# Two-chunk attention blocks: first AV phases ahead of the second scores, from chunk 8 on, with later loads held back

## The chip, the cores and the metric

The kernel runs on one core of one Trainium2 chip. The metric is the device time of one execution in microseconds; the profile is one execution of its own, taken by the hardware profiler.

## The reference

Eight batches of eight heads with 576 positions and 64 channels: causal attention in which each position sees itself and the 63 before it, then, on the heads put side by side (4608 tokens of 512 channels), a gated feed-forward network with 1536 hidden units.

```python
scores = scale * np.matmul(q, k.transpose(0, 1, 3, 2))
mask = (rel >= 0) & (rel < window)            # rel = i - j, window = 64
attn = softmax(np.where(mask, scores, -1e9))
x = (attn @ v) laid out as (B * S, H * D)     # 4608 x 512
out = (silu(x @ w_gate) * (x @ w_val)) @ w_out
```

Inputs and output are float32; the kernel works in bfloat16 with float32 sums.

## The kernel before

**Order of work.** The program is written out by hand as one list of operations, each for one engine; `_Graph` (L32) finds from the tiles read and written which operation waits for which, and gives each engine its operations in the order of the list. A wait on the own engine is made only where the list asks for it with `after=`. A DMA takes one of 16 lanes of its queue (POOL and SP have 16 each, ACT 8) and waits for the lane's DMA before it.

**Tiling.** The 4608 tokens are 36 chunks of 128 tokens. Four chunks make one of nine feed-forward groups c of 512 tokens. A chunk n passes through:

- `load` (L307), on POOL: q and k of chunk n into rings `qn`, `kn` of eight, v into a ring `va` of ten, from float32 to bfloat16 on the way. A chunk that crosses a batch's border takes two DMAs for each.
- `T` (L349), on SP: DMA transposes of kn and qn into rings `kT`, `qT` of eight chunks. Chunks 4 to 9 are loaded by `load2` and transposed on TensorE by `T2` instead.
- scores: `Sx` (L600) gives `Sb` for chunks under 18 (24 small matmuls: L419, L423) and `Sk` from 18 on (16 or more: L468); each takes a pair of PSUM banks, and two exponentials on ACT write `pt` (L431, L477). `Sm` (L436) multiplies `pt` by the mask on DVE.
- attention times v, AV: `AVa` (L511) takes a pair of banks; `AVp` (L606) issues phase 0 or phase 1, some 32 matmuls of 64x64 each way (L535 in `AVmm` for chunks under 18, L498 in `AVk` from 18 on). Phase 1 adds to what phase 0 left in the same banks and is given `after=done[0]`, the operation of phase 0 of the same chunk. `AVn` (L571) divides by the row sums on DVE (L577, L580) into `xb`.
- `X` (L623): transposes `xb` into `xT`, by an SP DMA (L632), or with "act" by TensorE and an ACT copy.
- `F` (L682): for hidden tile f, four matmuls with the gate weights and four with the value weights (L702), a tanh on ACT (L708) and two DVE operations (L710, L712) into `hT`. All F of group c need xT of its chunks 4c to 4c + 3; some F of groups 0 and 1 do a half or a quarter of the tokens.
- `O` (L718): twelve matmuls of 512 columns (L738), a copy on ACT and the store on ACT's queue. `O2` (L723) does the same as two halves of 256 columns in two banks, copied by ACT and DVE, with the store called later.

**PSUM.** There are eight banks. At first two fixed rings serve; once `lru` is set (L930, just before chunk 12's block) `bank` takes the least recently touched bank and `pair` the neighbouring pair whose later touch is oldest. "Touched" counts operations of the list.

**Blocks.** `B(n)` (L590), a single-chunk block: phase 0 of n, scores of n + 1, phase 1 of n. Chunks 8 to 15 go through it (L907 to L937), chunk 8's and 17's scores stand alone (L901, L947), and F, O and X lie between the blocks. `B2(n)` (L609), a two-chunk block: scores n + 2, phase 0 of n, scores n + 3, phase 0 of n + 1, then phase 1 and AVn of n, then of n + 1, then the masks. The loop for groups 3 to 8 (L950) calls B2 at u = 0 and u = 2, each after two F and an O2; after it come the store, X of both chunks, the transposes T of k for n + 4 and n + 5 and of q for n + 5 and n + 6, the loads of q and k for n + 7 and n + 8, then of v for n + 2 and n + 3. Loads wait only for buffers and lanes, so POOL runs far ahead of the other engines.

Of the kernel before, what the change touches and what calls it, by code (L numbers as in the profile page):

```python
# [11 lines left out]
NFC = T // 512  # L12
# [141 lines left out]
class _Kernel:  # L154
# [149 lines left out]
        g.op("dve", lambda e: e.tensor_copy(k[64:128, 0:64], m[64:128, 64:128]), reads=["mask"], writes=[("kmask", 1)])  # L304
        g.op("dve", lambda e: e.tensor_copy(k[64:128, 64:128], m[64:128, 0:64]), reads=["mask"], writes=[("kmask", 2)])

    def load(self, n, what="kqv"):  # L307
        if n >= NCH:
            return
        parts = list(self.segs(128 * n, 128))  # L310
        for x in what:
            src = {"k": self.k, "q": self.q, "v": self.v}[x]
            if x == "v":
                dst, nm, i = self.va[n % self.NV], "va", n % self.NV
            else:
                i = n % self.NQ
                dst = (self.kn if x == "k" else self.qn)[i][:, :].rearrange("p (h d) -> p h d", h=H)
                nm = x + "n"
            for j, (r, b, s, L) in enumerate(parts):
                d = dst[r:r + L, :, 0:64]  # L320
                a = src[b, :, s:s + L, :].rearrange("h p d -> p h d")
                ks = [(nm, i, j)] if len(parts) > 1 else [(nm, i, 0), (nm, i, 1)]
                self.g.op("pool", lambda e, d=d, a=a: e.dma_start(d, a), writes=ks, dma=True)  # L323

    def load2(self, st, x):
        src, dst = (self.k, self.ks2[st % 2]) if x == "k" else (self.q, self.qs2[st % 2])
# [281 lines left out]

    def B2(self, n):  # L609
        ss = [m for m in (n + 2, n + 3) if m < NCH]  # L610
        st = []
        for i in range(2):
            if i < len(ss):
                self.Sx(ss[i])
            st.append(self.AVa(n + i))
            self.AVp(st[i], 0)
        for a in st:
            self.AVp(a, 1)
            self.AVn(a)
        for m in ss:  # L620
            self.Sm(m)
# [96 lines left out]
    def O(self, c, u):  # L718
        io = (4 * c + u) % self.NO
        self.Omm(c, u, 0, 512, "act", [("ost", io), ("osth", io)])  # L720
        self.store(c, u)

    def O2(self, c, u):  # L723
        io = (4 * c + u) % self.NO
        self.Omm(c, u, 0, 256, "act", [("osth", io)])
        self.Omm(c, u, 256, 512, "dve", [("ost", io)])

    def Omm(self, c, u, lo, hi, eng, wr):
        g = self.g
        ih = c % self.NH  # L730
        hT = self.hT[ih]
        ost = self.ost[(4 * c + u) % self.NO]
        OB, ok = self.bank("f")
        n = hi - lo

        def pe(e):
            for f in range(NF):
                r = e.matmul(OB[:, 0:n], hT[:, f, 128 * u:128 * u + 128], self.Wo[:, f, lo:hi],  # L738
                             start=(f == 0), stop=(f == NF - 1))
            return r  # L740

        g.op("pe", pe, reads=self.hTk(ih) + [("Wo", f) for f in range(NF)], writes=[ok])
        self.copy(eng, ost[:, lo:hi], OB[:, 0:n], [ok], wr)
# [57 lines left out]
    def late_loads(self):  # L801
        self.load2(4, "k")
        self.load2(4, "q")
        self.load_wo(0, 6)
        self.load_wo(6, 12)
        self.load(10, "kq")
        self.load(8, "v")
        self.load(11, "kq")
        self.load(9, "v")

    def Tkq(self, n):
        self.T(n, "k")
# [2 lines left out]
    def build(self):  # L815
        F, S, AV, X, T2, O = self.F, self.S, self.AV, self.X, self.T2, self.O
        self.loads()
        self.banks("a", [4, 5, 6, 7, 0, 1, 2, 3, 4, 5, 0, 1, 2, 3, 4, 5, 6, 7, 0, 1, 2, 3, 4, 5, 6, 7, 6, 7])
        self.warm(72, n=80)
        self.first_T(("dve", "act"))  # L820
        s0 = self.Sa(0)
        T2(0, "q", ("act", "dve"))
        self.Sbias(s0)
        self.warm(2)
        self.Sb(s0)
        s1 = self.Sa(1, True)
        self.Sb(s1)
        T2(1, "k", ("dve", "act"))
        T2(1, "q", ("dve", "act"))
        self.early_loads()  # L830
        s2, s3 = self.Sa(2), self.Sa(3)
        a0, a1, a2, a3 = self.AVa(0), self.AVa(1), self.AVa(2), self.AVa(3)
        self.AVs(a0)
        self.shift(1, 0, "dve")
        self.AVn(a0)
        self.Sbias(s2)
        self.Sb(s2)
        self.AVs(a1)
        self.AVn(a1)
        self.Sbias(s3)  # L840
        self.Sb(s3)
        X(0, "dve", "a")
        X(1, "dve", "a")
        self.warm(1, j=2)
        self.AVs(a2)
        self.AVn(a2)
        self.AVs(a3)
        self.AVn(a3)
        F(0, (0, 1), 0, 256)
        X(2, "act", "a")  # L850
        X(3, "act", "a")
        F(0, (2, 3), 0, 256)
        F(0, (0, 1), 256, 512)
        self.banks("a", [4, 5, 6, 7])
        self.init_va(4, self.NV)
        self.more_loads()
        F(0, (2, 3), 256, 512)
        F(0, (4,))
        F(0, (5,))
        F(0, (6,))  # L860
        T2(2, "k", ("act", "act"))
        T2(2, "q", ("act", "act"))
        self.late_loads()
        F(0, (7,))
        S(4)
        F(0, (8,))
        self.B(4)
        F(0, (9,))
        X(4, "act")
        T2(3, "k", ("act", "act"))  # L870
        F(0, (10,))
        a5 = self.AVa(5)
        self.AVmm(a5, 0)
        T2(3, "q", ("act", "act"))
        self.AVmm(a5, 1)
        self.AVn(a5)
        F(0, (11,))
        X(5, "act")
        F(1, (0, 1), 0, 128)
        S(6)  # L880
        F(1, (0, 1), 128, 256)
        F(1, (2, 3), 0, 256)
        self.B(6)
        F(1, (4, 5), 0, 256)
        X(6, "act")
        T2(4, "k", ("act", "act"))
        F(1, (6, 7), 0, 256)
        a7 = self.AVa(7)
        self.AVmm(a7, 0)
        T2(4, "q", ("act", "act"))  # L890
        self.AVmm(a7, 1)
        self.AVn(a7)
        self.load(12, "kq")
        self.load(10, "v")
        for n in range(10, 12):
            self.Tkq(n)
        O(0, 0)
        X(7, "act")
        self.load(13, "kq")
        self.load(11, "v")  # L900
        S(8)  # L901
        O(0, 1)
        self.load(14, "kq")
        self.load(12, "v")
        self.Tkq(12)
        F(1, (0, 1), 256, 512)
        self.B(8)  # L907
        X(8)
        self.Tkq(13)
        F(1, (8,))  # L910
        self.load(15, "kq")
        self.load(13, "v")
        F(1, (2, 3), 256, 512)
        self.B(9)
        X(9)
        self.Tkq(14)
        F(1, (9,))
        O(0, 2)
        F(1, (10,))
        self.B(10)  # L920
        self.load(16, "kq")
        F(1, (4, 5), 256, 512)
        F(1, (11,))
        X(10, "act")
        self.B(11)
        self.load(17, "kq")
        O(0, 3)
        X(11, "act")
        F(1, (6, 7), 256, 512)
        self.lru = True  # L930
        self.init_kmask()
        for u in range(4):
            n = 12 + u
            for m in ((18,), (19, 20), (21,), (22,))[u]:
                self.load(m, "kq")
            self.load(n + 2, "v")
            self.B(n)  # L937
            X(n)
            for m in ((15, 16), (17,), (18,), (19,))[u]:
                self.Tkq(m)  # L940
            if u == 3:
                self.T(20, "q")
            F(2, (3 * u,))
            F(2, (3 * u + 1,))
            O(1, u)
            if u == 3:
                self.Sx(17)  # L947
                self.Sm(17)
            F(2, (3 * u + 2,))
        for c in range(3, NFC):  # L950
            for u in range(4):
                n = 4 * c + u + 4
                F(c, (3 * u,))
                F(c, (3 * u + 1,))
                two = n < NCH and u % 2 == 0
                if two:
                    self.O2(c - 1, u)
                elif n < NCH or u < 3:
                    O(c - 1, u)
                if two:  # L960
                    self.B2(n)
                    self.store(c - 1, u)
                    X(n)
                    X(n + 1)
                    for m in (n + 4, n + 5):
                        self.T(m, "k")
                    for m in (n + 5, n + 6):
                        self.T(m, "q")
                    for m in (n + 7, n + 8):
                        self.load(m, "kq")  # L970
                    for m in (n + 2, n + 3):
                        self.load(m, "v")
                F(c, (3 * u + 2,))
                if n >= NCH and u == 3:
                    O(c - 1, u)
        for u in range(3):
            O(NFC - 1, u)
        self.O_last(NFC - 1, 3)
        self.g.emit()
# [42 lines left out]
```

## Time and profile before

| what | us |
|---|---|
| median of three runs (lowest, highest) | 334.62 (333.92, 335.17) |
| the profiled execution | 335.11 |
| its span, first to last instruction | 333.1 |
| TensorE (PE) busy | 324.1 |
| weight loads (PEld) busy, beside PE | 181.7 |
| VectorE (DVE) busy | 207.2 |
| ScalarE (ACT) busy | 134.4 |
| POOL busy | 107.0 |

| DMA queue | packets | MB | share of 16 engines |
|---|---|---|---|
| q0, loads from POOL | 109008 | 18.62 | 78.2% |
| q1, transposes from SP and the first load | 42848 | 10.63 | 22.2% |
| q10, stores from ACT | 5456 | 9.57 | 8.1% |
| q8, instructions | 28 | 0.46 | 0.6% |

TensorE's granted clock is 1.00 throughout. Starts in the trace are counted from the span's start. A row of a timeline names start, length, engine, line, operation, tiles and count; the bracket at its end is the idle time before it and what ended that, where "issue" means that the profile names nothing. A row of a windows table names the stretch and its length, then busy time and count for each engine asked for, the granted clock, the mean share of the DMA engines and GB/s.

### The profile page before, as it was taken

Reading aid. Unit: us, or ns where it says so; the run is one execution under the profiler, and the core shown is the slowest. Engines: PE = TensorE matmul, PEld = TensorE weight load, DVE = VectorE, ACT = ScalarE, POOL = GpSimd, SP = SyncE. Lnnn points to the kernel's source line nnn. Section 1 sums busy time; section 2 is a strip of 40 time slices with the busy share of each in tenths; the row PEclk is TensorE's granted clock in tenths of the full one; section 3 lists DMA queues with packets and bytes.
Section 4 is the critical chain, followed back from the end, with each engine's and each line's share of the span. In section 5 each row is a group of like instructions: output and inputs, shape, how many; then the busy total and the mean of one; then the engine's idle time right before and its main releaser. Section 6 shows DMA issues by size and latency. Waiting matters only on the chain.

```text
span 333.1 us, 8426 instructions
## 1 busy us (share of the span) xinstructions
PE 324.1 (97%) x3615; PEld 181.7 (55%) x3615; DVE 207.2 (62%) x365; ACT 134.4 (40%) x243; POOL 107.0 (32%) x137
## 2 busy tenths in 40 slices
PE   7899999998999999999999999999999999999996
PEld 6585586655544455555555464646464646444444
DVE  4676884666666658575757575757666667555520
ACT  2645764644433444342424242434342422233221
POOL 8899977644226320607060830100000000000000
PEclk9999999999999999999999999999999999999999
DMA  9999999999999998969996997541423211100012
GB/s 139 178 191 185 177 200 155 173 137 153 173 161 176 158 147 118 151 92 134 124 150 104 137 166 112 81 96 50 110 63 81 59 40 49 48 31 33 31 61 97
DMA packets 157348, 39.34 MB, mean 118 GB/s; under 512 B 144384, under 2 KB 152832, under 8 KB 157312
## 3 DMA queue, kind: packets, MB, share of 16 engines
q0 software_dynamic: 109008, 18.62, 78.2%
q1 hardware_dynamic: 42848, 10.63, 22.2%
q10 hardware_dynamic: 5456, 9.57, 8.1%
q8 instruction: 28, 0.46, 0.6%
q14 instruction: 8, 0.07, 0.1%
HBM read 37.75 MB, written 9.44 MB: 142 GB/s over the span
## 4 chain that ended last, share of the span: by engine, by line
PE 92%; POOL 2%; DMA 2%; issue 1%; ACT 1%; DVE 1%; POOLq 0%
PE ps L702 56%; PE ps L738 28%; DMA va<-in_v_dram 2%; PE ps L498 2%; PE ps L535 2%; PE ps L468 2%; POOL vs L257 1%; PE ps L372 1%; PE ps L423 1%; PE ps L419 1%; PE ps L639 1%; POOL qs L332 1%; ACT kT L255 0%; ACT qT L255 0%; POOL ks L332 0%
## 5 line engine op out<-in xcount | busy, mean ns | idle before, releaser
L710 DVE SCALAR_TENSOR_TENSOR uu<-sig,ps 128x512 bf16<-128x512 bf16 (+1 forms) x109 | 74.0, 679 | 69.2 <-ACT sig L708 69.1
L702 PE MATMUL ps<-xT,Wg 128*128 128x512 bf16 (+2 forms) x488 | 111.4, 355 | 0.4 <-issue 0.4
L702 PE MATMUL ps<-xT,Wv 128*128 128x512 bf16 (+2 forms) x488 | 111.2, 355 | 0.0
L738 PE MATMUL ps<-Wo,hT 128*128 128x256 bf16 (+1 forms) x564 | 99.0, 329 | 1.3 <-issue 1.3
L708 ACT ACTIVATE sig<-ps 128x512 bf16<-128x512 f32 (+1 forms) x109 | 64.9, 596 | 79.2 <-PE ps L702 78.9
L738 PEld LDWEIGHTS ps<-Wo,hT 128*128 128x128 bf16 x564 | 54.9, 98 | 41.7 <-issue 1.8
L712 DVE SCALAR_TENSOR_TENSOR hT<-uu,ps 128x512 bf16<-128x512 bf16 (+1 forms) x109 | 74.3, 682 | 3.8
L702 PEld LDWEIGHTS ps<-xT,Wv 128*128 128x128 bf16 x488 | 47.1, 98 | 46.3
L702 PEld LDWEIGHTS ps<-xT,Wg 128*128 128x128 bf16 x488 | 44.8, 98 | 42.8 <-issue 0.8
L255 ACT ACTIVATE ost<-ps 128x512 f32<-128x512 f32 (+1 forms) x36 | 19.2, 532 | 83.3 <-PE ps L738 83.3
L323 POOL DMA_DIRECT2D kn<-in_k_dram x29 | 25.0, 869 | 72.8 <-DMA kT<-kn 68.0
L323 POOL DMA_DIRECT2D va<-in_v_dram x40 | 34.8, 893 | 19.6 <-PE ps L498 17.9
L323 POOL DMA_DIRECT2D qn<-in_q_dram x29 | 25.0, 872 | 10.9 <-DMA va<-in_v_dram 3.5
L580 DVE TENSOR_TENSOR xb<-ps,rc 128x512 bf16<-128x512 f32 x36 | 24.9, 692 | 1.2
L477 ACT ACTIVATE pt<-ps 128x512 bf16<-128x512 f32 x36 | 18.6, 602 | 11.6 <-PE ps L468 11.6
L431 ACT ACTIVATE pt<-ps 128x512 bf16<-128x512 f32 x36 | 19.4, 595 | 9.2 <-PE ps L423 8.8
L257 DVE COPY ost<-ps 128x256 f32<-128x256 f32 x11 | 4.7, 425 | 26.2 <-PE ps L738 26.2
L445 DVE TENSOR_TENSOR pt<-pt,mask 128x1024 bf16<-128x1024 bf16 x14 | 9.6, 684 | 8.6 <-ACT pt L431 8.6
L577 DVE RECIPROCAL rc<-ps 128x8 f32<-128x8 f32 x36 | 7.3, 203 | 7.6 <-PE ps L498 5.6
L445 DVE TENSOR_TENSOR pt<-pt,kmask 128x1024 bf16<-128x1024 bf16 x18 | 11.5, 683 | 0.0
L535 PE MATMUL ps<-va,pt 64*64 64x65 bf16 x448 | 8.9, 196 | 0.6 <-issue 0.5
L498 PE MATMUL ps<-va,pt 64*64 64x65 bf16 x544 | 9.1, 194 | 0.0
(59 smaller groups left out, 136.9 us busy)
## 6 DMA issues: line engine op xcount, KB each, us to landing
out_dram<-ost ACTq DMA_DIRECT2D x35, 256.0 KB, 3.0
va<-in_v_dram POOLq DMA_DIRECT2D x32, 128.0 KB, 7.8
kn<-in_k_dram POOLq DMA_DIRECT2D x23, 128.0 KB, 11.3
qn<-in_q_dram POOLq DMA_DIRECT2D x23, 128.0 KB, 10.8
Wg<-in_moe_w_gate_dram POOLq DMA_DIRECT2D x6, 256.0 KB, 7.4
Wv<-in_moe_w_val_dram POOLq DMA_DIRECT2D x6, 256.0 KB, 6.8
Wo<-in_moe_w_out_dram POOLq DMA_DIRECT2D x2, 768.0 KB, 14.4
qs<-in_q_dram POOLq DMA_DIRECT2D x3, 256.0 KB, 6.7
```

The lines of the kernel that those rows point to most:

```text
L255: self.g.op("act", lambda e: e.activation(d, a, ACTF.Copy), reads=reads, writes=writes)
L323: self.g.op("pool", lambda e, d=d, a=a: e.dma_start(d, a), writes=ks, dma=True)
L431: g.op("act", lambda e, po=po, p=p: e.activation(po, sv[p], ACTF.Exp, scale=SCALE), reads=[bx[p][1]], writes=[pk[p]])
L445: self.g.op("dve", lambda e: e.tensor_tensor(pt, pt, m, ALU.mult), reads=pk + mk, writes=pk)
L477: g.op("act", lambda e, po=po, p=p: e.activation(po, sv[p], ACTF.Exp, scale=SCALE), reads=[bx[p][1]], writes=[pk[p]])
L498: x = e.matmul(av[64 * c:64 * c + 64, p, j, :], pt[rows, h, x0:x0 + 64], vv[rows, h, 0:65], start=first, stop=phase == 1, skip_group_check ...
L580: g.op("dve", lambda e: e.tensor_tensor(xo, av[:, :, :, 0:64], rb, ALU.mult), reads=bk + [("rc", ir)], writes=[("xb", ix, 0), ("xb", ix, 1)])
L702: r = e.matmul(bank[:, a * n:a * n + n], W[:, kk, f * 128:f * 128 + 128], xT[:, kk, lo:hi], start=(kk == 0), stop=(kk == NK - 1))
L708: g.op("act", lambda e, G=bank: e.activation(sig[:, 0:w], G[:, 0:w], ACTF.Tanh, scale=0.5), reads=[bk], writes=[("sig", i)])
L710: g.op("dve", lambda e: e.scalar_tensor_tensor(uu[:, 0:w], sig[:, 0:w], 1.0, G[:, 0:w], ALU.add, ALU.mult), reads=[("sig", i), gk], writes ...
L712: g.op("dve", lambda e: e.scalar_tensor_tensor(out, v3(uu), 0.5, v3(V), ALU.mult, ALU.mult), reads=[("uu", i), vk], writes=[("hT", ih, f) ...
L738: r = e.matmul(OB[:, 0:n], hT[:, f, 128 * u:128 * u + 128], self.Wo[:, f, lo:hi], start=(f == 0), stop=(f == NF - 1))
```

## The change

1. `B2` issues scores n + 2, phase 0 of n and of n + 1, then scores n + 3, then both second phases. It also keeps phase 0 of chunk n as `gate`.
2. `O2` takes its two banks as a pair.
3. Chunks 8 to 15 go through B2: scores 8 and 9 stand together, the blocks of 8 and 10 are written out in group 1's part, each after an O2, and the loop begins with group 2. Bank choice by age and the mask for later chunks (`init_kmask`) are set before O(0, 0).
4. Loads of q, k, v: chunks 12 and 13 (q, k) and 10 and 11 (v) move up into `late_loads`; later ones are given `after=gate`. In the loop the loads of v come ahead of those of q and k.

```diff
     def B2(self, n):
         ss = [m for m in (n + 2, n + 3) if m < NCH]
-        st = []
-        for i in range(2):
-            if i < len(ss):
-                self.Sx(ss[i])
-            st.append(self.AVa(n + i))
-            self.AVp(st[i], 0)
+        if ss:
+            self.Sx(ss[0])
+        st = [self.AVa(n), self.AVa(n + 1)]
+        for a in st:
+            self.AVp(a, 0)
+        self.gate = st[0][3][0]
+        if len(ss) > 1:
+            self.Sx(ss[1])
         for a in st:
             self.AVp(a, 1)
             self.AVn(a)
...
     def O2(self, c, u):
         io = (4 * c + u) % self.NO
-        self.Omm(c, u, 0, 256, "act", [("osth", io)])
-        self.Omm(c, u, 256, 512, "dve", [("ost", io)])
+        bx = self.pair()
+        self.held -= {b[1][1] for b in bx}
+        self.Omm(c, u, 0, 256, "act", [("osth", io)], bx[0])
+        self.Omm(c, u, 256, 512, "dve", [("ost", io)], bx[1])
```

In `build`, after the second phase of chunk 7, the new order is:

```python
        self.gate = a7[3][0]
        for n in range(10, 12):
            self.Tkq(n)
        self.lru = True
        self.init_kmask()
        O(0, 0)
        X(7, "act")
        S(8)
        S(9)
        O(0, 1)
        for n in (14, 15):
            self.load(n, "kq", self.gate)
        F(1, (0, 1), 256, 512)
        for n in range(12, 14):
            self.Tkq(n)
        F(1, (8,))
        self.O2(0, 2)
        self.B2(8)
        self.store(0, 2)
        X(8)
        X(9)
        for n in (12, 13):
            self.load(n, "v", self.gate)
        for n in (16, 17):
            self.load(n, "kq", self.gate)
        F(1, (2, 3), 256, 512)
        F(1, (9,))
        F(1, (4, 5), 256, 512)
        self.O2(0, 3)
        self.B2(10)
        self.store(0, 3)
        for n in (14, 15):
            self.Tkq(n)
        self.T(16, "q")
        self.load(18, "kq", self.gate)
        F(1, (10,))
        X(10, "act")
        F(1, (6, 7), 256, 512)
        X(11, "act")
        F(1, (11,))
        for c in range(2, NFC):
```

The loop's body is as before but for the loads:

```diff
+                    for m in (n + 2, n + 3):
+                        self.load(m, "v", self.gate)
                     for m in (n + 7, n + 8):
-                        self.load(m, "kq")
-                    for m in (n + 2, n + 3):
-                        self.load(m, "v")
+                        self.load(m, "kq", self.gate)
```

## The prediction

> **What bounds the kernel now.** I read the page's busy shares first, then its slices and the chain that ended last, and then the timeline and the windows around each stretch that the change touches.
>
> ```profile
> PE 324.1 (97%) x3615; PEld 181.7 (55%) x3615; DVE 207.2 (62%) x365; ACT 134.4 (40%) x243; POOL 107.0 (32%) x137
> ...
> PE   7899999998999999999999999999999999999996
> ...
> DMA  9999999999999998969996997541423211100012
> ...
> PE 92%; POOL 2%; DMA 2%; issue 1%; ACT 1%; DVE 1%; POOLq 0%
> ```
>
> TensorE is busy for 97% of the span and makes 92% of the chain, so only what lengthens or shortens its stream counts. The DMA row is the second thing to see: the transfer engines are full up to slice 16 (about 130 us) and nearly idle afterwards. The changed blocks of chunks 8 to 15 (62 to 117 us) lie in the full part, the loop's blocks from chunk 16 on in the idle part.
>
> A full TensorE can still stand. In the timeline of PE:
>
> ```profile
> 78.28 1.47 PE L738 MATMUL ps<-Wo,hT 128*128 128x512 bf16 x6
> 81.01 1.47 PE L738 MATMUL ps<-Wo,hT 128*128 128x512 bf16 x6 [1.26 <-issue]
> ...
> 119.40 0.38 PE L702 MATMUL ps<-xT,Wg 128*128 128x512 bf16 x1 [0.39 <-issue]
> ```
>
> The first stop is in the middle of one group of twelve matmuls, which waits for nothing of the program. Its predecessor is at 53.6 us, in the middle of a second AV phase. Up to these two points TensorE's trace has 1,729 and 2,497 records (matmuls, weight loads, waits): 768 apart, three times 256. The page's queue q8 (kind "instruction") has 28 packets of 16 KB for 7,331 such records, 262 each. One of those packets begins at 51.96 and one at 78.46, and TensorE resumes 2.3 and 2.55 us later. So these are **waits for the next block of 256 instructions**; starts of single matmuls put the second at 1.42 us above the usual pitch. The stop at 119 us is another kind: F(3, 0) needs xT of chunk 15, whose transpose by SP was issued at 112.25 and landed at 119.31; against the pitch it costs 0.55 us.
>
> **The change, part by part.** *Reordering B2.* Windows of PEld in the block of chunk 18 (us, busy, count):
>
> ```profile
> 142.49:143.55 1.06, 0.96 (x72) 1.00 0.18 11
> 143.55:143.63 0.08, 0.00 (x0) 1.00 0.00 0
> 143.63:143.89 0.26, 0.22 (x17) 1.00 0.00 0
> ```
>
> The empty row is the second AV phase of chunk 19, held by done[0] until the first phase of chunk 19 has drained; only chunk 18's second phase lies between. From start to start this gap is 0.13 to 0.17 us in the nine blocks of chunks 16 to 32, 1.38 in sum; an unforced one is 0.004. After the change the scores of n+3 and a phase lie between, so the wait goes: at most -1.35. What is late next: the four bank pairs of a block are used in the order scores, AV, scores, AV; now the second scores take the fourth pair, by the least-recently-touched rule that of O2. DVE's copy of O2's second half ends 0.53 us after the block's start (142.69 + 0.42), and with 0.05 us of signalling the pair is free at 0.58; scores (0.25) and two AV phases (0.13 each) with a switch bring TensorE there at about 0.52. I charge 0.06 a block, 0.5 in all: **-0.8**, bounds -1.35 and 0 (should the wait be as long as the one removed). The last block has no scores and stays.
>
> *Two-chunk blocks for 8 to 15.* Windows of PE: one single block, one lone scores group, one two-chunk block:
>
> ```profile
> 109.85:110.59 0.74, 0.74 (x57) 1.00 1.84 147
> 116.71:117.19 0.48, 0.48 (x26) 1.00 1.06 63
> 125.47:126.91 1.44, 1.44 (x98) 1.00 1.53 97
> ```
>
> Before: eight single blocks and two lone scores (8 and 17), 8 x 0.74 + 2 x 0.48 = 6.88. After: scores 8 and 9 together (0.48 + 0.25) and four blocks of 1.44 - 0.16 + 0.06 = 1.34: 6.09. Four more projections become O2, 24 half-width matmuls in 2.62 us for 12 in 2.59: +0.12. Sum **-0.67**; bounds -0.9 and -0.3.
>
> *The stop at 119 us.* X(14) and X(15) are now issued after the block of 14, two F and one O before F(3, 0), with about 7.3 us in hand beyond X(15)'s issue where 7.1 were short by a little; the loads then in flight are the question (a rival below). **-0.55**.
>
> *Loads.* POOL issues one load in 0.88 us; loads from 14 on now wait for a first AV phase, which on POOL delays all behind it. Needed dates: scores 10/11 at 66.9 (kT/qT 11 landed 64.4 in the profile), 12/13 at 76 (here about 73), 14/15 at 89 (about 86), so 2.5 to 4 us of cover; the order of SP (T 12 and 13, X 8 and 9, T 14 on) keeps them, and X(8), X(9), landing near 79, are needed by F(2, 0) at 83. If a transfer took 4 us longer, each such date would stop TensorE by what exceeds the cover. V of 12 and 13 is issued at 67 and needed at 89. Cost **0**, bounds 0 and +1.5. init_kmask's three small DVE copies and the bank rule move 30 us ahead beside a DVE that is 0.7 busy there: 0.
>
> *Instruction blocks.* This is the term that costs. The change packs TensorE's short instructions: a two-chunk block has 224 of them in 1.3 us, O2 has 48 where O has 24. Counting on from the stop at 53.6 (record 1,729; the next borders are at 1,985, 2,241, 2,497), I take a block as asked for 296 records before its border, since from 125 us on the packets begin 0.4 to 1.9 us after that record; between 45 and 115 us they begin 3.9 to 6.1 us after it (mean 5.0), and at the stops use came 2.3 to 2.5 us later still. The profiled kernel took 10.9 us over the 296 records before 2,241 and 6.7 over those before 2,497, which was 1.4 too few. Laid out with the new order, the request for 2,241 falls eight instructions into O2(0, 2), at 64.6; then come the block of 8 (224 instructions), one F and border 2,241 at 69.8: 5.2 us against 6.2 to 8.6. I take the delay of the row nearest in time (4.36, the packet at 66.8): 4.4 + 2.4 + 0.2 = 7.0, a stop of 1.8. The next, 2,497, lies inside the block of 10, 7.1 us after that stop's end; its packet, counted from there as the one at 86.43 came 5.4 after the resumption at 81.01, needs 6.2 to 8.6, 7.5 in the middle: 0.5. Together 2.3 instead of 1.42: **+0.9**, bounds -1.4 (no stop) and +3.8.
>
> The Trainium skill, "Runtime: NRT & Kernel Launch", section "Instruction fetch mechanics", says that instructions come in 16 KiB blocks of 256 through the sequencer's own DMA queue, and that the cost of crossing a border is mostly hidden. The block size agrees with the trace's 768 = 3 x 256; "mostly hidden" does not hold at 53.6 and 79.4 us, where 0.5 and 1.42 us show. By that sentence the two stops of the new order would be absent and the sum 2.3 lower.
>
> *Transposes beside loads:* +0.1 (below). **Sum**: -0.8 - 0.67 - 0.55 + 0.9 + 0.1 = -1.0. The profiled execution took 335.11 us, 333.1 of span and 2.0 around it; this makes 334.1. It lay 0.5 above the median of 334.62, so for a median I forecast **333.6**.
>
> **Rivals.** *A, instruction blocks arrive in time:* held-back loads leave the transfer queue emptier, and a packet begins within 1 us as it does after 125 us. For it: DMA is then idle from about 86 to 89 us. Against it: at 64 to 76 us the loads of 11, 14 and 15, four transposes and a store are still to move. 333.6 - 2.3 = 331.3.
>
> *B, slower: X collides with the held-back loads.* In the idle part the loads used to start after SP's kT transposes, some 8 us into a block's period; now they start at the first AV phase, 2.8 us before X(n+1). Landing of X's transposes (min/median/max), first 50 to 80 us, then 125 to 230 us:
>
> ```profile
> DMA to landing us min/median/max: 8.7/8.8/9.0
> ...
> DMA to landing us min/median/max: 2.4/3.1/5.9
> ```
>
> In blocks with u = 2, F(c+1, 0) needs X(n+1) 7.3 us after its issue. It decides from that point: at 9.0 us each of the four blocks that still load (14, 18, 22, 26) stops for 1.7, +6.8: 340.3. Against it: the nearest rows beside fresh loads are 5.9 (X at 195.7 us) and 6.8 (qT at 185.2), inside the 7.3. The Trainium skill, "DMA: Bandwidth & Descriptors", section "Queues, rings and completion order", has each engine go round between its queues packet by packet, which speaks against a transpose waiting for whole loads; 8.8 against 3.1 us in the trace shows that it waits for much all the same.
>
> *C, the reordering gives nothing:* the second scores wait for O2's copies as long as the phase did. 333.6 + 0.8 = 334.4.
>
> *D, slower: both instruction blocks come at the late end,* 3.5 and 1.7 us of stop instead of 1.8 and 0.5: 333.6 + 2.9 = 336.5.
>
> **How the numbers follow.** Forecast 0.47 (332.3 to 335.0 of its own), A 0.25, C 0.10, D 0.10, B 0.08. The range runs from A's 331.3, less 0.3 for a run's scatter, to 335.6, part of the way to D: 331.0 to 335.6 leaves out B, most of D and A's tail. 0.5%, about what a measurement of this kernel can tell from no change, is 1.67 us: faster (below 332.95) is A and 0.10 of the forecast, 0.35; slower (above 336.3) is B and half of D, 0.13; the same 0.52.
>
> **What would show it.** Right: in two-chunk blocks no empty stretch of PEld before the last AV phase, and blocks near 1.30 to 1.34 us; F(3, 0) without a stop; a stop near 70 us 256 records before the old one at 2,497. Wrong: no "issue" stop between 64 and 80 us (A); stops at F(4, 0), F(5, 0) ended by xT's transposes (B); an empty stretch ahead of the second scores (C); stops over 3 us (D).

## The result and the profile after

| | median us (lowest, highest) | runs | ratio to before (95%) |
|---|---|---|---|
| before | 333.99 (333.09, 335.54) | 20 | |
| after | 335.83 (333.88, 337.56) | 20 | 1.0047 (1.0026 to 1.0067) |

The kernel became slower by 0.5%; 333.6 was forecast, range 331.0 to 335.6. Its executions spread over 3.7 us where those of before spread over 2.5. They come in two kinds: ten have a mean granted clock of 0.990 to 0.995 and a median of 336.8 us, ten one of 0.999 or 1.00 and a median of 334.3. The profiled execution of the changed kernel, one of the first kind, took 336.66 us with a span of 334.9, 1.8 more than before.

The page of the changed kernel, busy shares and slices:

```profile
PE 325.5 (97%) x3663; PEld 186.9 (56%) x3663; DVE 210.0 (63%) x369; ACT 132.9 (40%) x243; POOL 107.1 (32%) x137
...
PEclk9999999989999999999999999999999999999999
...
DMA  9999999999999898979896959596949352100012
```

The number of matmuls rose by 48, as it must for four more O2, and no engine became the bound. New is the 8 in the row PEclk, the clock that TensorE was granted. The DMA row shows the held-back loads: the full part now has gaps and reaches further into the loop.

The timeline of PE around that 8, in the changed kernel:

```profile
69.15 0.82 PE L704 MATMUL ps<-xT,Wv 128*128 128x256 bf16 x6
72.25 0.39 PE L704 MATMUL ps<-xT,Wv 128*128 128x256 bf16 x2 [2.29 <-issue]
```

The stop stands in the middle of a group of sixteen matmuls, at record 2,241 of TensorE's stream, the border that the prediction named, 69.7 us where it had said 69.8. The packet of instructions began 5.05 us after the record taken for its request and TensorE resumed 2.55 us after the packet's start: 2.34 us above the pitch where 1.8 had been forecast. The prediction had no line for what follows. Windows of PE (us, busy and count, granted clock, DMA share, GB/s):

```profile
66.71:70.12 3.41, 3.26 (x129) 1.00 1.61 179
70.12:73.53 3.41, 1.27 (x7) 1.00 2.14 143
73.54:76.95 3.41, 3.41 (x14) 0.50 3.40 133
```

From 73.54 to 76.95 us the clock is granted at one half. In that row PE is busy throughout, with 14 matmuls, and those of 512 columns start 427 ns apart where they started 216 apart before it. It does in 3.41 us what it else does in 1.71: **1.7 us** on the path for a stop that was already over. The cut into rows of 3.41 us is the profile's own: the clock's record before it lasts 68.27 us, 20 times 3.413.

The two profiled executions, term by term in us (from starts of single instructions in both traces):

| | forecast | measured |
|---|---|---|
| order inside B2, nine blocks from 16 on | -0.8 | -0.70 |
| two-chunk blocks for 8 to 15, with four more O2 | -0.67 | -0.31 |
| stop before F(3, 0) | -0.55 | -0.55 |
| X late at F(5, 0) and F(6, 0) | +0.1 | +0.53 |
| standing for instruction blocks at 64 to 80 us | +0.9 | +0.92 |
| clock at one half afterwards | not thought of | +1.71 |
| up to O(0, 0) | 0 | +0.18 |
| sum | -1.0 | +1.78 |

The sum is the difference of the spans. It holds for these two executions: the term of the clock is missing in the ten whose clock did not fall. Two windows of PE, the blocks of chunks 18 and 8 in the changed kernel, show the first two terms:

```profile
144.37:145.67 1.30, 1.30 (x90) 1.00 0.00 0
...
66.84:68.27 1.43, 1.43 (x115) 1.00 1.48 194
```

The first took 1.40 before. The second has replaced two single blocks of 0.74, and had been put at 1.34.

### The profile page after: what moved, and what is told of

It is laid out like the page before. It is cut to its first block, busy times and chain, and to the rows that moved or that the text cites. A ratio compares the mean times of both kernels' runs of the same rounds, so it can differ in the third digit from the quotient of the medians.

```text
span 334.9 us, 8502 instructions
## 1 busy us (share of the span) xinstructions
PE 325.5 (97%) x3663; PEld 186.9 (56%) x3663; DVE 210.0 (63%) x369; ACT 132.9 (40%) x243; POOL 107.1 (32%) x137
## 4 chain that ended last, share of the span: by engine, by line
PE 91%; POOL 3%; DMA 2%; issue 1%; ACT 1%; DVE 1%; POOLq 0%
PE ps L704 55%; PE ps L742 28%; DMA Wv<-in_moe_w_val_dram 2%; PE ps L468 2%; PE ps L498 1%; PE ps L535 1%; POOL va L323 1%; PE ps L419 1%; PE ps L372 1%; POOL qs L332 1%; POOL Wg L338 0%; PE ps L423 0%; PE ps L641 0%; ACT kT L255 0%; ACT qT L255 0%
## 5 line engine op out<-in xcount | busy, mean ns | idle before, releaser
L742 PEld LDWEIGHTS ps<-Wo,hT 128*128 128x128 bf16 x612 | 59.7, 98 | 36.4
L255 ACT ACTIVATE ost<-ps 128x512 f32<-128x512 f32 (+1 forms) x36 | 18.3, 509 | 77.3 <-PE ps L742 77.3
L257 DVE COPY ost<-ps 128x256 f32<-128x256 f32 x15 | 6.4, 425 | 32.2 <-PE ps L742 32.2
L423 PE MATMUL ps<-qT,kT 64*64 64x64 bf16 x288 | 7.9, 195 | 0.5 <-issue 0.5
L535 PE MATMUL ps<-va,pt 64*64 64x65 bf16 x448 | 7.5, 194 | 0.5 <-issue 0.4
```

The costliest lines, as they stand in the source:

```text
L255: self.g.op("act", lambda e: e.activation(d, a, ACTF.Copy), reads=reads, writes=writes)
L535: x = e.matmul(av[64 * c:64 * c + 64, p, j, :], pt[rows, h, 64 * c:64 * c + 64], vv[rows, h, 0:65], start=first, stop=phase == 1, skip_gro ...
```

## The experiments

Theory 1: the loss is the wait for a block of instructions at 70 us and the halved clock that it brings; what the prediction said of the rest holds. Theory 2: the held-back loads cost the time. Theory 3: the new order of the blocks costs it. In the names, a_ is a variant of the changed kernel and b_ of the kernel before. The medians of before in the four sets were 334.1, 334.0, 334.7 and 334.0.

**Moving the borders, changed kernel.** Five F of group 0 do their matmuls in halves, 80 instructions more, so that each border of 256 lies 80 earlier in the program:

```diff
-                for a, f in enumerate(fs):
+                for a, f, lo2, hi2 in ((a, f, h * n // cut, (h + 1) * n // cut) for a, f in enumerate(fs) for h in range(cut)):
...
-        F(0, (4,))
+        F(0, (4,), cut=2)
```

> The changed kernel with 80 more TensorE instructions ahead of it: in group 0 the F of hidden tiles 4 to 8 do their matmuls in halves of 256 columns (40 more matmuls, 40 more weight loads, the same columns). Nothing else moves, but every border of 256 instructions now lies 80 instructions earlier in the program. Theory 1 (the loss is the wait for instruction blocks and the halved clock behind it): laid out with 7.4 us from request to use, no border between 40 and 110 us is late any more; the stops at 53.8 (0.5 us) and 69.7 us (2.3 us) and the halved clock after it (1.7 us) go, the split costs 0.1 to 0.2: 335.8 - 4.3 = 331.5 us, within 0.8. Theory 2 (the held-back loads cost the time) and theory 3 (the new order of the blocks costs it): the stop is not what matters, 335.5 to 336.0 us.

Measured 332.0 us, ratio 0.9935 (0.9913 to 0.9956), 3.8 below the changed kernel. The timeline of PE after the block of chunk 8, and at F(3, 0):

```profile
68.07 1.04 PE L704 MATMUL ps<-xT,Wv 128*128 128x256 bf16 x8
69.16 0.81 PE L704 MATMUL ps<-xT,Wg 128*128 128x512 bf16 x3
69.81 1.03 PE L704 MATMUL ps<-xT,Wv 128*128 128x512 bf16 x4
...
117.84 0.38 PE L704 MATMUL ps<-xT,Wg 128*128 128x512 bf16 x1 [1.18 <-DVE uu L712]
```

There is no stop where the changed kernel has its own, in the group of the first line, which there broke into six and two; nor is there any from 40 to 110 us. The clock stays at 1.00, and none of the six executions has a lower mean. Gates and order are still in, so theories 2 and 3 are out as causes of the loss. What the sum of 4.3 lacks stands in the last line: F(3, 0), due 4.9 us earlier than in the changed kernel, waits 1.3 us for X(15), whose transpose took 8.5 us beside the loads. The name in the bracket is of DVE; DVE had been done with its operation before, and what landed at 117.75 was X(15).

**Moving the borders, kernel before.**

```diff
-        self.warm(72, n=80)
+        self.warm(76, n=80)
...
-        F(0, (4,))
+        F(0, (4,), cut=2)
```

> The kernel before with 56 more TensorE instructions ahead: three F of group 0 in halves (48) and four more warm-up matmuls (8). Theory 1: its two stops for instruction blocks (0.5 us at 53.6, 1.4 us at 79.4) go, nothing else changes: 334.0 - 1.8 = 332.2 us, within 0.6. So the changed kernel without its stops would be about 0.7 us ahead of this one. Theories 2 and 3: 333.8 to 334.2 us.

Measured 332.8 us, ratio 0.996 (0.9946 to 0.9975). Both stops are gone; the one at F(3, 0), which waits for a transpose by DMA, grew from 0.55 to 0.97 us. Without stops for instructions the changed kernel (332.0) would be 0.8 us ahead of this one.

**Moving the borders the other way.**

```diff
-        self.warm(72, n=80)
+        self.warm(48, n=120)
```

> The changed kernel with 48 TensorE instructions fewer ahead of it: 48 warm-up matmuls of 120 columns in place of 72 of 80. Every border of 256 instructions lies 48 later in the program. Theory 1: the stop at 69.7 moves to about 73 us and shrinks to 1 us, and a new one of 3 to 4 us stands inside the block of chunk 10 at 77 us, with the clock halved for at least one stretch of 3.4 us: 336.5 to 339.0 us. Theories 2 and 3: 335.8 us, and nothing moves.

Measured 338.76 us, ratio 1.0131 (1.0088 to 1.0174). Timeline and windows of PE:

```profile
73.20 0.39 PE L704 MATMUL ps<-xT,Wv 128*128 128x256 bf16 x2 [1.31 <-issue]
81.83 0.39 PE L535 MATMUL ps<-va,pt 64*64 64x65 bf16 x13 [4.37 <-issue]
```

```profile
77.58:80.99 3.41, 0.00 (x0) 1.00 1.82 128
81.00:84.41 3.41, 2.25 (x18) 0.50 1.75 196
84.41:87.82 3.41, 3.41 (x17) 0.50 1.47 90
```

The stop went where the counting put it, one of 1.3 us and a new one of 4.4 inside the block of chunk 10, and the clock fell for two stretches: 2.25 us busy in the first of them did not bring it back. Twenty-four warm-up matmuls fewer, in the first 7 us, cost 2.9 us.

**The order alone, and the order undone.** b_order is the kernel before with the new `B2` and `O2`; a_oldorder is the changed kernel with

```diff
-        if ss:
-            self.Sx(ss[0])
-        st = [self.AVa(n), self.AVa(n + 1)]
-        for a in st:
-            self.AVp(a, 0)
-        self.gate = st[0][3][0]
-        if len(ss) > 1:
-            self.Sx(ss[1])
+        st = []
+        for i in range(2):
+            if i < len(ss):
+                self.Sx(ss[i])
+            st.append(self.AVa(n + i))
+            self.AVp(st[i], 0)
+        self.gate = st[0][3][0]
```

> The kernel before with only the new order inside B2 and the pair of banks for O2; single-chunk blocks for 8 to 15 and the loads as before. Theory 1: the nine blocks from chunk 16 on shorten by 0.7 us in sum as they do in the changed kernel, the stop at 79.4 us stays: 334.0 - 0.7 = 333.3 us, within 0.4. Theory 3 (the order costs): 334.5 us or more. The theory of the prediction said 333.2.

Measured 333.72 us, ratio 0.9995 (0.9977 to 1.0012): unclear, since its stops vary by as much as the order is worth.

> The changed kernel with the old order inside B2 (scores, phase 0, scores, phase 0), all else as changed. Theory 1: 13 blocks are longer by 0.08 each, 1.0 us in all, the stop near 69.7 us and the halved clock stay: 336.6 us, within 0.8. Theory 3: it is faster than the changed kernel, near 334.5 us. Theory 2: as theory 1.

Measured 336.52 us, ratio 1.0065 (1.0041 to 1.0089), 0.7 above the changed kernel; the stop stood 2.8 us and the clock was halved. Nine of its twelve executions have a lowered mean clock, against ten of twenty of the changed kernel, so the 0.7 is not the order's alone; the three others have a median of 334.6 for 334.3 there. Where no instruction block is late, the order's worth can be read: b_order_shift56 is b_order with the 56 additional instructions.

> The kernel before with the new order in B2 and the 56 additional instructions, so without stops for instruction blocks: the order's own worth. If it is 0.7 us, as the windows of the nine blocks say, 332.8 - 0.7 = 332.1 us, within 0.4; a later X(15) can take back up to 0.4. If the order is worth nothing: 332.8 us.

Measured 332.12 us, ratio 0.9938 (0.9917 to 0.996), 0.7 below b_shift56 as its blocks say. It also lies only 0.1 above a_shift80: with the borders out of the way, two-chunk blocks from chunk 8 on and held-back loads are worth next to nothing together.

**The loads not held back.**

```diff
-                self.g.op("pool", lambda e, d=d, a=a: e.dma_start(d, a), writes=ks, dma=True, after=gate)
+                self.g.op("pool", lambda e, d=d, a=a: e.dma_start(d, a), writes=ks, dma=True)
```

> The changed kernel without the waits of the loads on a first AV phase: each load is issued as soon as its buffer and lane are free, in the changed order. Theory 1: the stop for instructions near 69.7 us stays, 2 to 3 us with the clock halved after it; the two stops for xT late in the loop (0.4 us at 188.8, 0.2 at 223.0) go: 335.3 us, within 1.2. Theory 2 (the held-back loads cost the time): 333.5 us or less, and no stop near 70 us.

Measured 335.68 us, ratio 1.0044 (1.0023 to 1.0065). The stop near 69.7 stood 2.6 us, with the halved clock behind it; the two late stops for xT are gone. So the gates are not the cause, and taking them away gains nothing that shows.

**The price of a stop, by itself.** In the quiet part of the kernel before, F(6, 4) waits for k copies on POOL:

```diff
+    def pause(self, k):
+        a, b = self.vs[0], self.vs[1]
+        o = self.last
+        for i in range(k):
+            o = self.g.op("pool", lambda e: e.tensor_copy(a[0:64, :, 0:64], b[0:64, :, 0:64]), after=o)
+        return o
...
-                F(c, (3 * u + 1,))
+                F(c, (3 * u + 1,), after=self.pause(2) if (c, u) == (6, 1) else None)
```

> The disputed cost by itself: the kernel before with a pause put into its quiet part. In group 6, F of tile 4 waits for a chain of two POOL copies that starts when F of tile 3 has ended; DMA and all other engines are idle enough. TensorE stands some 1.6 us. If a stop costs what it stands: 334.0 + 1.6 = 335.6 us, and no drop of the granted clock. If any stop halves the clock: 337.3 us.

Measured 335.72 us, ratio 1.0044 (1.0024 to 1.0064): 1.7 above before for a stop of 1.56, the clock at 1.00.

> The same with four POOL copies: TensorE stands some 3.0 us. Theory 1: the clock is granted at half for 3.4 us afterwards, which takes 1.7 us more: 334.0 + 3.0 + 1.7 = 338.7 us, within 0.5. If a stop costs what it stands: 337.0 us.

Measured 337.91 us, ratio 1.0091 (1.0056 to 1.0126). The six executions lie in two groups, two at 336.2 and 336.3 and four from 337.8 to 338.6, 1.9 apart in the mean. The lower two have a mean clock of 1.00, three of the upper four 0.995; the fourth, 337.77, has 1.00 on record, which stays unexplained. The profiled one is of the upper group:

```profile
231.34:234.75 3.41, 1.02 (x5) 1.00 0.53 105
234.75:238.16 3.41, 3.41 (x10) 0.50 1.37 112
```

> The pause in the quiet part with three POOL copies: TensorE stands some 2.2 us, between the pause that never lowered the granted clock in the profile (1.6) and the one that did (2.9). If the clock falls when enough of one stretch of 3.41 us is idle, and the stretches run free of the program, some executions lie near 334.0 + 2.2 = 336.2 us and others near 337.9 us. If it depends on the pause's length alone, all lie at one of the two.

Measured 336.29 us, ratio 1.0053 (1.0033 to 1.0073): all seven between 335.3 and 336.9, so no two groups in the times; the expectation was wrong in that. Two of the seven, 336.55 and 336.86, do have a mean clock of 0.995, the others 1.00. Its profile, cut on the grid that the clock's record at its end gives:

```profile
230.18:233.59 3.41, 1.50 (x7) 1.00 0.68 112
233.59:237.00 3.41, 3.25 (x16) 1.00 0.88 96
```

This stretch with 1.50 us of busy PE did not lower the clock; stretches with 1.27 (after), 1.07 (a_nogate), 1.02 (b_stop4) and 0.66 (a_oldorder) did. There is no limit of busy time between them, though: in a_shift_late, below, a stretch with 1.83 us, most of it short matmuls, lowered it too. What the clock goes by stays open. A stop of some 2 to 3 us can fall inside one stretch or across two; that would explain why the clock falls in one execution and not in another, but where the stretches of the executions without a profile lay is not known.

**Emptying DMA at the critical moment.** The loads of q and k for 14 and 15 wait for chunk 8's first AV phase, 67.65 us in place of 53.54:

```diff
-        for n in (14, 15):
-            self.load(n, "kq", self.gate)
         F(1, (0, 1), 256, 512)
...
         X(9)
+        for n in (14, 15):
+            self.load(n, "kq", self.gate)
```

> The changed kernel with the loads of q and k for chunks 14 and 15 held back further, until the first AV phase of chunk 8 (67 us in place of 53.5): from 64 to 68 us only the tail of v 11, two transposes and a store are left for DMA. TensorE's stream is the same. If the packet of instructions is late because of the traffic beside it: it begins 1 to 3 us after its request in place of 5, the stop near 70 us shrinks to under 1 us, the clock is not halved, 335.8 - 3.2 = 332.6 us, or up to 1.5 more if q and k of 14 and 15 now come late at 89 us. If the packet's delay belongs to the request itself: the stop stays above 1.5 us, 335 us or more.

Measured 333.5 us, ratio 0.9973 (0.9954 to 0.9993). Shares of the DMA queues from 64.8 to 68.8 us, changed kernel first:

```profile
q0 software_dynamic: 1369, 0.17, 65.9%
q1 hardware_dynamic: 1373, 0.33, 65.4%
q10 hardware_dynamic: 145, 0.26, 20.3%
```

```profile
q1 hardware_dynamic: 1683, 0.41, 89.7%
q10 hardware_dynamic: 204, 0.36, 32.6%
q0 software_dynamic: 108, 0.01, 5.0%
q14 instruction: 1, 0.01, 0.5%
```

The loads (q0) are out of the way, transposes and the store move up into their place, and the packet begins 4.1 us after its request in place of 5.05: the stop is 1.8 us, the clock is not halved (the matmuls of 512 columns behind the stop start 216 ns apart, and none of the ten executions has a lowered mean), and the time falls by 2.3 us. The next border now stops TensorE as well, for 0.6 us at 79.6 us. Neither answer came as written. The loads in flight account for about 1 us of the delay; whether transposes and store account for the other 3 was not tried. What 1 us was worth, though, shows how the price jumps where the stop becomes short enough.

**The two small waits that were left.** a_shift_late is a_shift80 with the loop's loads behind X:

```diff
+                F(c, (3 * u + 2,))
+                if two:
                     for m in (n + 2, n + 3):
-                        self.load(m, "v", self.gate)
+                        self.load(m, "v", self.last)
                     for m in (n + 7, n + 8):
-                        self.load(m, "kq", self.gate)
-                F(c, (3 * u + 2,))
+                        self.load(m, "kq", self.last)
```

> The changed kernel with the 80 additional instructions of a_shift80, and the loop's loads no longer tied to the first AV phase: they wait for the V matmuls of the block's last F, some 2.5 us later, so that X goes ahead of them. In a_shift80 X(15) took 8.5 us and F(3, 0) stood 1.3 us for it. If the loads beside it make X late: X lands in 5 us or less, that stop goes, 332.0 - 1.3 = 330.7 us, within 0.6. If it is the transposes among themselves and the store that make it late: 332.0 us and the stop stays.

Measured 331.69 us, ratio 0.9928 (0.9901 to 0.9954), 0.3 below a_shift80. X(14) landed in 2.4 us where it took 6.4 in a_shift80, X(15) in 6.3 where it took 8.5, and the stop at F(3, 0) is gone, so the loads beside X made it late. The gain is smaller than the stop: two scores now wait, 0.33 and 0.21 us by their brackets, the second for a transpose of q, presumably because a later load makes a later T:

```profile
158.61 0.42 PE L468 MATMUL ps<-qT,kT 64*64 64x128 bf16 x16 [0.33 <-issue]
159.58 0.41 PE L468 MATMUL ps<-qT,kT 64*64 64x128 bf16 x21 [0.21 <-DMA qT<-qn]
```

Its slowest execution (333.68) is the profiled one, in which the clock was halved at 15.93 us. Windows of PE there:

```profile
12.52:15.93 3.41, 1.83 (x66) 1.00 1.53 191
15.93:19.34 3.41, 3.05 (x53) 0.50 1.45 197
```

Ahead of it lies a stop of 1.42 us at 13.1 us, for which the profile names nothing, at record 449, seven times 256 before 2,241. The changed kernel stood 0.51 us there. This border comes ahead of the F that were cut, so nothing here moved it.

```diff
-        self.Omm(c, u, 0, 256, "act", [("osth", io)], bx[0])
-        self.Omm(c, u, 256, 512, "dve", [("ost", io)], bx[1])
+        self.Omm(c, u, 0, 256, "dve", [("osth", io)], bx[0])
+        self.Omm(c, u, 256, 512, "act", [("ost", io)], bx[1])
```

> a_shift_late with the two copies of O2 exchanged: DVE takes the first half, ACT the second, which ends sooner (0.385 us in place of 0.425). If the second scores wait for the copy of O2's second half, as the gap of 0.12 to 0.17 us before them says, each of 13 blocks shortens by 0.04 to 0.06 us: a_shift_late - 0.6 us, within 0.3. If that gap is the switch between AV and scores: the same time as a_shift_late.

Measured 331.08 us, ratio 0.99 (0.9879 to 0.9921), another 0.6 below, and the fastest kernel of the study: 1.0% under before, 4.8 us under the changed kernel. The time came as the first answer had it, but the trace does not show its mechanism. One block of each kernel, a_shift_late first: first AV phases, second scores, copy of O2's second half.

```profile
193.01 0.42 PE L498 MATMUL ps<-va,pt 64*64 64x65 bf16 x32
193.41 0.42 PE L468 MATMUL ps<-qT,kT 64*64 64x128 bf16 x16
192.87 0.42 DVE L257 COPY ost<-ps 128x256 f32<-128x256 f32 x1 [1.45 <-PE ps L742]
...
190.50 0.42 PE L498 MATMUL ps<-va,pt 64*64 64x65 bf16 x32
190.91 0.42 PE L468 MATMUL ps<-qT,kT 64*64 64x128 bf16 x16
190.36 0.38 ACT L255 ACTIVATE ost<-ps 128x256 f32<-128x256 f32 x1 [2.89 <-PE ps L742]
```

The copy now ends 0.04 us sooner, and the second scores follow the AV phases at the same distance as before. In eight of the 13 blocks the gap between the last AV matmul and the second scores is the same to 0.01 us in both traces, and in sum it is no smaller. So the second scores did not wait for that copy there, and where the 0.6 us come from stays open.

## Why the prediction was wrong

- **The step that failed** is the term for instruction blocks: "Together 2.3 instead of 1.42: +0.9". The place was right, border 2,241 at 69.7 us. The standing, 2.34 us against 2.3, was right by luck: the stop of 1.8 came out at 2.34, since the packet took 5.05 us and not the 4.4 chosen (the mean that the prediction gives is 5.0), and the 0.5 at 2,497 (0.4 by its own 7.5 less 7.1) did not come at all. What failed is that the term priced a stop at the time that TensorE stands. The profile of before could not show otherwise: its 1.42 us fell across two stretches of the clock's grid, with 2.91 and 2.65 us busy, and left the clock alone. The stop of 2.34 left 1.27 us busy in one stretch and took 1.71 more. a_shift80 (both gone), a_shiftm48 (both moved) and the pauses in the quiet part show it; so do the executions of the changed kernel itself, 334.3 us in the median where the mean clock is 0.999 or more and 336.8 where it is lower.
- On this the Trainium skill, "TensorE: Matmul & The Clock Gate", table under "Why this matters for your kernels", advises no gaps over about 3 us, and its section "What's actually happening" tells of free-running windows of 3413 ns. The length of the windows agrees with the trace (3.41 us). The advice is too mild for this case: 2.34 us were enough.
- **Order inside B2**: -0.70 for -0.8. The old wait is gone. Left is a gap of 0.10 to 0.20 us between the AV phases and the second scores, which was 0.06 to 0.10. That this is the wait for O2's second copy, as the prediction had it, is not shown: with the copies exchanged the gap stayed as it was.
- **Two-chunk blocks for 8 to 15**: the mechanism was right, the size wrong, -0.31 for -0.67. The block was put at 1.34 us and took 1.43: the price came from a block with 16-matmul scores from 18 on, and with 24-matmul scores for n + 3 the gap from AV to scores is 0.165 us in all four.
- **Stop before F(3, 0)**: gone as forecast, but by luck: X(15) landed at 121.24 us, 7.1 us after its issue, and F(3, 0) began at 121.36. In a_shift80 the stop is back with 1.3 us and in a_shiftm48 with 1.2, on the mechanism of rival B (8.5 and 7.9 us of landing against the 7.3 that it named).
- **Rival B** itself cost 0.38 us at 188.8 and 0.16 at 223.0, for 0.1 charged; X landed in 5.3 to 7.5 us in the loop, 2.4 to 5.9 before. **Rival A** was wrong, the packet came late. **Rival D** had the right sign for a reason that it did not know.
- "Cost 0" for the **dates of the loads** held: no score and no AV phase of the changed kernel waits for one.
- The **number** came closer than the change it stands for: the forecast was 1.0 us under the 334.62 of three runs, and twenty runs put before at 333.99, so the change forecast was -1.0 us and the one measured +1.8. The chance of "slower by over 0.5%" was 0.13; the measured 0.47% is still within the middle case, just outside the range.

## What to carry to other kernels

Count TensorE's instructions between two points, not only its time: packing short ones beside busy transfers can bring a border of 256 before its block has arrived, and a few instructions more or less at the start move all borders. A stop of the bound engine costs more than it lasts once it empties most of one 3.41 us stretch, so price a stop of 2 us or more with the chance of a halved clock behind it. A small gain in every block is only worth measuring once such a jump is out of the way: at 333.72 the new order showed nothing, and behind moved borders it was worth 0.7.

## What the runs showed that was not expected

- The price of a stop jumps: pauses of 1.56 and 2.24 us cost 1.7 and 1.6 us (336.29 less the 334.69 of its own set, in which three of the twelve executions of before had a lowered clock), one of 2.9 us cost 2.2 or 4.1.
- The time of a whole kernel moved by 6.8 us (332.0 to 338.76) with nothing changed but the number of instructions ahead of the same stream.
- With the loads gone from DMA, the block of instructions still came 4.1 us after its request at 65 us, against 0.4 to 1.9 late in the kernel.
